# Pooled attention with a feed-forward layer: from the fourth chunk on, every engine's order is written out

## The chip, the cores and the metric

The kernel runs on one core of a Trainium2 chip. The metric is device microseconds of that core for one execution; lower is better. TensorE (PE) multiplies matrices into PSUM, VectorE (DVE) and ScalarE (ACT) copy and compute, GpSimd (POOL) computes in SBUF alone, and SyncE (SP) issues DMAs. Each engine works through its own list of instructions in order: one that waits for a semaphore holds back all that stand behind it on that engine.

## The reference

```python
# 8 batches, 8 heads, 576 positions, 64 columns a head; k and v are averaged over groups of 8 positions
k_p = k.reshape(B, H, Sp, pool, D).mean(axis=3)
v_p = v.reshape(B, H, Sp, pool, D).mean(axis=3)
scores = scale * np.matmul(q, k_p.transpose(0, 1, 3, 2))
scores = scores - np.max(scores, axis=-1, keepdims=True)
attn = np.exp(scores)
attn = attn / (np.sum(attn, axis=-1, keepdims=True) + 1e-09)
out = np.matmul(attn, v_p)
# 4608 tokens of 512 columns, then w_in 512 x 2048 and w_out 2048 x 512
x = out.transpose(0, 2, 1, 3).reshape(B * S, H * D)
h = x @ w_in
return np.maximum(0.01 * h, h) @ w_out
```

## The kernel before

The 4608 tokens are worked through in nine chunks of 512 columns, numbered 0 to 8. Each factor of a product is held as a high and a low part, and three matmuls (high by high, high by low, low by high) stand for one product at full precision.

Chunks 0 to 2 multiply x by w_in directly. From chunk 3 on (`FAST = 3`) a product of two 2 x 2 block matrices is made from seven block products instead of eight. The function `pair` does this for two column blocks of w_in at a time, eight pairs to a chunk. Its names: `chain` (in the bank `pv`) and `left` and `right` (halves of the bank `pu`) are PSUM areas; `held` and `h` are SBUF copies and sums of them. A product's six matmuls are lines 1168 to 1170. ACT copies `chain` to `held` (L1196, L1203, L1209), DVE adds `held` to `left` or `right` (L1198, L1210, L1220), and ACT and DVE split the result into `gh` and `gl` (L1189, L1191). The product with w_out is cut into tiles of 128 tokens, three matmuls each (`m2_tile`, L1074 to L1076, called fills here); `pair` takes them from a list and puts them between block products. Four block products read sums of weight blocks that stand in DRAM: `load_sums` fetches them, 512 KB at a time, into three buffers in turn (`streamed`, L1130, issued by ACT).

Attention for later chunks runs beside the products of a chunk, piece by piece. For a tile of 128 positions and a group of four heads: scores (`pss`, L560, PE), maxima (L568, DVE), four exponentials (L572, ACT), sums and reciprocals (L592, L593, DVE), normalised rows (`at`, L600 to L610, POOL). SP writes them to DRAM (`rows<-at`, L626) and reads them back in another layout (`blocks<-rows`, L635); DVE transposes `blocks` in squares of 32 (L643), ACT and DVE split them (L647 to L650), and PE multiplies them by v (`pa`, L692 to L697). `turn_x` then builds from x the seven operands of the next chunk (B11, B21, T2, T1, T3, T4, B22; a cast on ACT, L1161, and a difference on DVE, L1162, each).

The order on PE is the order of the code (`manual_schedule` for PE alone): `tick()` is called after each step of a pair and takes the next attention unit from a list, evenly spread over the chunk. The order on DVE, ACT, POOL and SP is set by the scheduler of the tile layer from its own estimates of time, with a few `issue_after` hints.

Of the kernel before, what the change touches and what calls it, by code (L numbers as in the profile page):

```python
# [20 lines left out]

@with_exitstack
def tile_pooled_attention_ffn(
# [9 lines left out]
    nc = tc.nc  # L35

# [14 lines left out]


# [57 lines left out]

# [50 lines left out]


# [30 lines left out]
    def convert(i, f):  # L193
# [3 lines left out]
        def head():  # L197
# [7 lines left out]

            after = casts[max(0, len(casts) - BEHIND)] if casts else anchor.get("act")
            with tc.issue_after(after.ins) if after else nullcontext():
# [3 lines left out]
            with tc.issue_after(behind.ins) if behind else nullcontext():  # L211
# [14 lines left out]

# [112 lines left out]
    def get_keys():  # L339
        for i in range(2):  # L340
            for c in range(2):
                r, y = 64 * i + 32 * c, slice(32 * c, 32 * c + 32)
# [9 lines left out]
    def turn_keys(b):  # L352
        kT = keys_values(b)[0]
        with tc.issue_after(anchor["gl"].ins):
            nc.vector.transpose(kblocks, kblocks)
# [6 lines left out]
    def load_v(b):  # L362
# [9 lines left out]
        def finish():  # L372
            pooled(nc.vector if b == 1 else nc.gpsimd, sums[:, 0:2], raws[0], P)
            with tc.issue_after(anchor["dve"].ins) if b == 0 else nullcontext():
# [6 lines left out]
    def raw_steps(b):  # L381
# [3 lines left out]
        def load(n):  # L385
# [4 lines left out]
            if n == 2:  # L390
                if b > 2:
                    put_keys(st["ks"])
# [15 lines left out]
        def add(n):  # L408
# [45 lines left out]
    def load_piece(b, j):  # L454
# [3 lines left out]
        for half in range(2):  # L458
            qb = two.tile([P, 2, PMAX], F32, tag="q", name=f"qb{b}_{j}_{half}")
            for h in range(4 * half, 4 * half + 4):  # L460
                for c in range(2):
# [5 lines left out]
            q_of[b, j, half] = qb  # L467
# [26 lines left out]
    def place_v(b, sums, rem):  # L494
        _, v_hi, v_lo, _ = keys_values(b)
        behind = [anchor[x] for x in ("gl", "gh")] if b == 1 else []
        with ExitStack() as order:
            for x in behind:
                order.enter_context(tc.issue_after(x.ins))
# [141 lines left out]
    def p_moved(b, j, g, ab):  # L641
        with tc.issue_after(anchor["gl"].ins):
# [117 lines left out]
    def attention(b):  # L760
# [34 lines left out]
        def step(kind, n):  # L795
            def f():
# [4 lines left out]
                with tc.issue_after(behind) if behind else nullcontext():  # L801
# [22 lines left out]
        def lv():  # L824
            if b == 1:
                with tc.issue_after(anchor["gl"].ins):
# [202 lines left out]


# [33 lines left out]
    def m2_tile(k, t):  # L1064
# [5 lines left out]
        if first:  # L1070
            accs[t] = ps_acc.tile([P, DM], F32, tag=f"acc{t}", name=f"acc{n}_{t}")
# [52 lines left out]
    def load_sums(q):  # L1124
# [5 lines left out]
        nc.scalar.dma_start(t.bitcast(F32), sums[q % len(sums)])  # L1130
# [33 lines left out]
    def product(c, p, out, a, b, start):  # L1164
        w, x = weights_of(c, p, a), operand[c, b]
        for kk in range(2):
# [3 lines left out]
            nc.tensor.matmul(out, w[1][kk], x[:, 0, kk], start=False, stop=kk == 1, **args)  # L1170

    def pair(n, c, p, at, fills):
# [5 lines left out]
        held = wts.tile([P, 3, HALF], F32, tag="w0_15", name=f"held{nm}")  # L1178
        h = wts.tile([P, 2, CH], F32, tag="w0_11", name=f"h{nm}")

        def fill(times=1):
            for _ in range(times):
                fills.pop(0)()

        def done(i, f, at):
            g = h[:, i, :]
            gh = three.tile([P, CH], F32R, tag="gh", name=f"gh{nm}_{f}")
            gl = three.tile([P, CH], F32R, tag="gl", name=f"gl{nm}_{f}")
            casts.append(nc.scalar.copy(gh, g))  # L1189
            anchor["gh"] = casts[-1]  # L1190
            anchor["gl"] = nc.vector.tensor_tensor(gl, g, gh.bitcast(F32), op=ALU.subtract)  # L1191
            gs[at] = gh, gl
            fills.extend(lambda t=t: m2_tile(at, t) for t in range(NT))

        product(c, p, chain, "A11", "B11", True)
# [3 lines left out]
        yield  # L1199
        fill(1 if p == 0 and c == FAST else 2)  # L1200
        yield
        product(c, p, chain, "S2", "T2", False)
        nc.scalar.copy(held[:, 1], chain)  # L1203
        product(c, p, right, "S1", "T1", True)
        yield
        fill(1 if p == 0 and c == FAST else 2)
        yield
# [3 lines left out]
        fill()  # L1211
        yield
        fill(2)
        yield
# [3 lines left out]
        done(1, 2 * p + 1, at + 1)  # L1218
        product(c, p, right, "S4", "B22", False)
        nc.vector.tensor_tensor(h[:, 0, HALF:], held[:, 1], right, op=ALU.add)  # L1220
        yield
        nc.scalar.activation(h[:, 0, :], h[:, 0, :], AF.Prelu, alpha=0.01)
        done(0, 2 * p, at)
        fill()
        yield
# [10 lines left out]
    def store(n, c, t, a):  # L1236
        if n == len(runs) - 1:
# [11 lines left out]
            return  # L1249
        o = five.tile([P, DM], F32, tag="o", name=f"o{n}_{t}")  # L1250
# [28 lines left out]
    def convert_to(n):  # L1279
        nonlocal stepped  # L1280
        while stepped < min(int(n), len(steps)):
            steps[stepped]()
            stepped += 1

# [50 lines left out]
    for n, (c, fs) in enumerate(runs):  # L1335
        us = list(units[n])
# [27 lines left out]
        if quick:  # L1364
            for p in range(NF // 2):
# [28 lines left out]
        if c == FAST - 1:  # L1394
            for m in range(4, len(NAMES)):
                turn_x(FAST, m)
            for qn in range(len(STREAM)):
                load_sums(qn)
    while fills:
# [33 lines left out]
```

## Time and profile before

| what | value |
|---|---|
| median of 3 runs | 1014.76 us (1010.26 to 1019.28) |
| the profiled execution, own time | 1018.58 us |
| its span, first to last instruction | 1016.7 us |
| start of chunk 3 (first block product) | 373.1 us |
| PE busy, share of the span | 914.8 us, 90% |
| DVE, ACT, POOL busy | 505.4, 498.7, 226.4 us |
| mean granted clock of TensorE | 0.971 |

The page gives busy times; the windows view cuts them by stretch, so that a chunk can be compared with the work in it. PE's matmuls overlap, so the length of one is not its cost: the distance between the starts of two that follow each other is. A waits view names, for each wait, the instruction that ended it, and the timeline shows the instructions of one engine in order of time.

### The profile page before, as it was taken

To read this page: it belongs to the slowest core of one execution; us is meant where nothing else is said; L and a number is where in the kernel's file an instruction comes from. 1 tells how busy PE (TensorE), PEld (TensorE's weight loads), DVE (VectorE), ACT (ScalarE), POOL (GpSimd) and SP (SyncE) were. 2 spreads that over 40 slices of the span, in tenths; PEclk is the share of its full clock that TensorE was granted. 3 is DMA by queue.
4 is the path that set the end of the run, shared out by engine and by line. 5 is a ranking of instruction groups with operands and counts; after the bars stand their busy time and mean duration, and the time that the engine had idled before them with its cause. 6 is when DMAs were issued, how large, how long until landed. Compare 5 with 4: busy or idle time off the path is not lost.

```text
span 1016.7 us, 15236 instructions
## 1 busy us (share of the span) xinstructions
PE 914.8 (90%) x5132; PEld 790.8 (78%) x5132; DVE 505.4 (50%) x1105; ACT 498.7 (49%) x1542; POOL 226.4 (22%) x366
## 2 busy tenths in 40 slices
PE   4988999998989997889979688878998899999998
PEld 3867788887768876778868577767877789898997
DVE  5798666244756654344445353443545444444222
ACT  4897755254434444434544344543555445444333
POOL 3022100434355411222113221134121111100000
PEclk9899999999989999899999898998999999999999
DMA  9995422334355927785578746887379636835442
GB/s 171 268 284 172 123 71 63 88 107 120 106 188 134 187 79 186 163 172 133 160 173 177 160 125 167 174 178 157 109 187 183 139 125 168 173 110 175 135 118 71
DMA packets 276694, 152.05 MB, mean 150 GB/s; under 512 B 229448, under 2 KB 240712, under 8 KB 276616
## 3 DMA queue, kind: packets, MB, share of 16 engines
q1 hardware_dynamic: 258760, 87.63, 39.4%
q10 hardware_dynamic: 17856, 63.45, 20.6%
q8 instruction: 41, 0.67, 0.3%
q14 instruction: 37, 0.30, 0.1%
HBM read 120.21 MB, written 30.82 MB: 149 GB/s over the span
## 4 chain that ended last, share of the span: by engine, by line
PE 49%; DMA 20%; SPq 8%; ACT 8%; DVE 7%; POOL 4%; issue 3%; ACTq 0%; DVEq 0%; POOLq 0%
PE acc L1074 8%; PE acc L1075 8%; PE acc L1076 7%; DMA blocks<-rows 6%; DMA rows<-at 4%; PE pv L1169 3%; PE pv L1168 3%; PE pv L1170 3%; ACT e L572 2%; PE pu L1168 2%; SPq L463 2%; PE ph L1050 2%; PE ph L1052 2%; PE ph L1051 2%; DMA vremraw<-in_v_dram 2%
## 5 line engine op out<-in xcount | busy, mean ns | idle before, releaser
L1074 PE MATMUL acc<-w,gh 128*128 128x512 f32 x576 | 235.3, 409 | 8.2 <-DVE o L1255 8.2
L1075 PE MATMUL acc<-w,gh 128*128 128x512 f32 x576 | 229.7, 399 | 0.0
L1076 PE MATMUL acc<-w,gl 128*128 128x512 f32 x576 | 228.1, 396 | 0.0
L1074 PEld LDWEIGHTS acc<-w,gh 128*128 128x128 f32 x576 | 111.1, 193 | 25.3 <-DVE o L1255 5.7
L572 ACT ACTIVATE e<-pss,red 128x72 f32<-128x72 f32 x320 | 98.5, 323 | 65.3 <-DVE red L568 64.2
L1076 PEld LDWEIGHTS acc<-w,gl 128*128 128x128 f32 x576 | 110.3, 191 | 25.1
L1075 PEld LDWEIGHTS acc<-w,gh 128*128 128x128 f32 x576 | 111.2, 193 | 14.3
L600 POOL TENSOR_TENSOR at<-e,red 128x128 f32<-128x128 f32 x100 | 42.4, 445 | 261.8 <-DVE red L593 137.1
L1168 PE MATMUL pv<-T,streamed 128*128 128x256 f32 x288 | 84.7, 294 | 9.7 <-ACT held L1196 6.5
L1191 DVE TENSOR_TENSOR gl<-h,gh 128x512 fp32r<-128x512 f32 x96 | 68.1, 713 | 40.7 <-ACT gh L1189 39.9
L1169 PE MATMUL pv<-T,streamed 128*128 128x256 f32 x288 | 82.2, 285 | 0.0
L1170 PE MATMUL pv<-T,streamed 128*128 128x256 f32 x288 | 81.9, 284 | 0.0
L1050 PE MATMUL ph<-x,w 128*128 128x512 f32 x192 | 79.2, 412 | 0.7 <-DVE gl L1060 0.7
L1052 PE MATMUL ph<-x,w 128*128 128x512 f32 x192 | 76.8, 400 | 0.6 <-DVE w L221 0.6
L1051 PE MATMUL ph<-x,w 128*128 128x512 f32 x192 | 76.7, 400 | 0.0
L1168 PEld LDWEIGHTS pv<-T,streamed 128*128 128x128 f32 x288 | 55.6, 193 | 18.5 <-ACT held L1196 9.3
L572 ACT ACTIVATION_READ_ACCUMULATOR e<-pss,red 128x1 f32 x320 | 66.3, 207 | 0.0
L1189 ACT CAST gh<-h 128x512 fp32r<-128x512 f32 x96 | 59.4, 624 | 10.1 <-DMA blocks<-rows 8.2
L1168 PE MATMUL pu<-T,streamed 128*128 128x256 f32 x96 | 30.0, 313 | 35.2 <-DVE h L1198 34.9
L1210 DVE TENSOR_TENSOR h<-held,pu 128x256 f32<-128x256 f32 x48 | 19.8, 412 | 83.5 <-ACT held L1209 83.4
L1169 PEld LDWEIGHTS pv<-T,streamed 128*128 128x128 f32 x288 | 55.6, 193 | 4.3
L1209 ACT COPY held<-pv 128x256 f32<-128x256 f32 x48 | 17.9, 374 | 78.4 <-PE pv L1170 78.4
(208 smaller groups left out, 2013.3 us busy)
## 6 DMA issues: line engine op xcount, KB each, us to landing
streamed<-sums ACTq DMA_DIRECT2D x120, 512.0 KB
w_bits<-in_moe_w_in_dram SPq DMA_DIRECT2D x16, 512.0 KB
w_bits<-in_moe_w_out_dram SPq DMA_DIRECT2D x16, 512.0 KB
sums<-sums SPq DMA_DIRECT2D x32, 256.0 KB
out_dram<-o SPq DMA_DIRECT2D x31, 256.0 KB
rows<-at SPq DMA_DIRECT2D x40, 192.0 KB
blocks<-rows SPq DMA_DIRECT2D x40, 120.0 KB
v0raw<-in_v_dram SPq DMA_DIRECT2D x16, 256.0 KB
```

The lines of the kernel that those rows point to most:

```text
L572: ins = nc.scalar.activation(e[:, h, :], scv[:, h, :], AF.Exp, bias=mx[:, h : h + 1], accum_out=sm[:, h : h + 1],)
L1050: nc.tensor.matmul(ph, w[:, 0, ks], xh[kk], start=kk == 0, stop=False)
L1051: nc.tensor.matmul(ph, w[:, 0, ks], xl[kk], start=False, stop=False)
L1052: nc.tensor.matmul(ph, w[:, 1, ks], xh[kk], start=False, stop=kk == NK - 1)
L1074: nc.tensor.matmul(a, gh[:, r], hi, start=first, stop=False)
L1075: nc.tensor.matmul(a, gh[:, r], lo, start=False, stop=False)
L1076: nc.tensor.matmul(a, gl[:, r], hi, start=False, stop=last)
L1168: nc.tensor.matmul(out, w[0][kk], x[:, 0, kk], start=start and kk == 0, stop=False, **args)
L1169: nc.tensor.matmul(out, w[0][kk], x[:, 1, kk], start=False, stop=False, **args)
L1170: nc.tensor.matmul(out, w[1][kk], x[:, 0, kk], start=False, stop=kk == 1, **args)
L1189: casts.append(nc.scalar.copy(gh, g))
L1191: anchor["gl"] = nc.vector.tensor_tensor(gl, g, gh.bitcast(F32), op=ALU.subtract)
```

## The change

From the first pair of chunk 3 on, DVE, ACT, POOL and SP are in manual order too. The list of units and `tick()` are not used there. Attention, the building of operands and the stores are cut into small tasks. A task names the tasks that it must follow and by how many places, and what it costs on ACT, DVE or SP; a pair has 15 places, `work` is called at each, and emits every task that is due and for which that place has room. A pair's own copies and additions are emitted at fixed places. The products' order in a pair is kept. `load_sums` is called in `product` and issued by SP instead of ACT; `held` and `h` are one buffer for all pairs; one Prelu reads two areas of `held`, and the split of the first column block is emitted in the next pair. `need` emits an operand's tasks just ahead of its product where they were not due yet. The core of the diff:

```diff
@@ load_sums @@
-        nc.scalar.dma_start(t.bitcast(F32), sums[q % len(sums)])
+        nc.sync.dma_start(t.bitcast(F32), sums[q % len(sums)])
@@ product @@
+        need(("T", c, b, 1))
...
+        if a in USED:
+            used = len(USED) * ((c - FAST) * (NF // 2) + p) + USED.index(a)
+            if used % 2:
+                load_sums(used // 2 + len(STREAM))
@@ pair @@
         product(c, p, chain, "A11", "B11", True)
         nc.scalar.copy(held[:, 0], chain)
+        if behind:
+            behind.pop(0)()
+        yield 1
         product(c, p, left, "A12", "B21", True)
-        nc.vector.tensor_tensor(h[:, 0, :HALF], held[:, 0], left, op=ALU.add)
+        nc.vector.tensor_tensor(held[:, 0], held[:, 0], left, op=ALU.add)
...
+    def may_go(name):
+        _, after, at, _, reader, cost = tasks[name]
+        if at > clock[0] or not all(gap_ok(x, d) for x, d in after):
+            return False
+        if reader and len(bankers) > 1 and not gap_ok(bankers[-2], 2):
+            return False
+        return all(room[x] > 0 for x in cost)
...
+    GRANTS = {
+        "act": {3: 9, 4: 6, 5: 6, 6: 6, 7: 6, 8: 2, 9: 6, 10: 6, 11: 6, 12: 3},
+        "dve": {1: 4, 3: 7, 4: 7, 5: 7, 6: 7, 7: 6, 8: 2, 9: 6, 10: 7, 11: 7, 12: 7, 13: 6},
+    }
+    FREE = (3, 4, 7, 8, 10, 11, 12, 15)
...
+    def work(at):
+        clock[0] += 1
+        for x, granted in GRANTS.items():
+            room[x] = min(room[x] + granted[at], 12) if at in granted and at not in (1, 3, 5, 9) else granted.get(at, 0)
+        room["sp"] = min(room["sp"] + 7, 7)
+        room["pe"] = int(at in FREE)
+        waiting_for = [x for x in tasks if x not in made]
+        for x in sorted(waiting_for, key=lambda x: tasks[x][3]):
+            if may_go(x):
+                emit(x)
...
+        task((*name, "put"), put, [((*name, "norm"), 3)], first=True, sp=5)
...
+        task((*name, "ld"), ld, [(x, 7) for x in last] + [((*before, "low"), 2)], first=True, sp=20)
+        task((*name, "turn"), turn, [((*name, "ld"), 13)], dve=11)
+        task((*name, "high"), high, [((*name, "turn"), 1)] + [((*before, "av", i), 1) for i in range(2)], act=7)
...
@@ the loop over chunks @@
+        if c == FAST:
+            by_hand.append(c)
+            order.enter_context(tc.manual_schedule(engines={e.engine for e in (nc.vector, nc.scalar, nc.gpsimd, nc.sync)}))
...
-                for i, _ in enumerate(pair(n, c, p, kf, fills)):
-                    if i in (3, 4, 5, 6, 7):
-                        used = len(USED) * ((c - FAST) * (NF // 2) + p) + i - 3
-                        if used % 2:
-                            load_sums(used // 2 + len(STREAM))
-                    tick()
+                for i in pair(n, c, p, kf, fills):
+                    work(i)
```

PE's list is the same up to the first block product of chunk 3. The other engines' lists up to there differ in the first three `streamed` loads, which now stand on SP, and in a few instructions of chunk 3 that the scheduler had drawn ahead into chunk 2 (transposes of q, parts of v) and that now stand behind. Three places of what follows show the change.

DVE in chunk 4, before: the transpose of the first `blocks` of batch 4's second piece, ahead of the third pair's second addition (`h4_2` is chunk 4, pair 2; L1198, L1210 and L1220 are the pair's additions).

```order
L355 STREAM_TRANSPOSE kblocks_119<-kblocks_119 128x384
L592 TENSOR_TENSOR red4_4_1_5142<-red4_4_1_5142,tiny_124 128x4
L1198 TENSOR_TENSOR h4_2_5151<-held4_2_5150,pu4_2_5149 128x256
L360 TENSOR_SCALAR kT_108<-kblocks_119 64x4x64
L360 TENSOR_SCALAR kT_108<-kblocks_119 64x4x8
L593 RECIPROCAL red4_4_1_5142<-red4_4_1_5142 128x4
L643 STREAM_TRANSPOSE blocks_134<-blocks_134 128x960
L1210 TENSOR_TENSOR h4_2_5151<-held4_2_5150,pu4_2_5149 128x256
```

The same transpose now (L1481), in chunk 4's second pair (the additions are L1225, L1246 and L1257 now):

```order
L1257 TENSOR_TENSOR held_3699<-held_3699,pu4_0_4887 128x256
L1211 TENSOR_TENSOR gl4_0_1_5043<-h_3700,gh4_0_1_5025 128x512
L1481 STREAM_TRANSPOSE blocks_134<-blocks_134 128x960
L1225 TENSOR_TENSOR held_3699<-held_3699,pu4_1_5055 128x256
L1211 TENSOR_TENSOR gl4_0_0_5076<-h_3700,gh4_0_0_5063 128x512
```

It still stands ahead of an addition (L1225), but 13 places behind the loads that it waits for.

SP at those loads, before: four `blocks<-rows` right behind two stores of rows.

```order
L626 DMA rows4_1_0_4891<-at4_4_0_5049 64x12x32
L626 DMA rows4_1_1_4987<-at4_3_1_5101 128x12x32
L635 DMA blocks_134<-rows4_1_0_4891 32x30x32 x4
L463 DMA qb5_1_0_5182<-in_q_dram 32x10x32 x4
L626 DMA rows4_1_1_4987<-at4_4_1_5168 64x12x32
```

Now the same loads are L650, with the `streamed` loads (L1144) between them and the stores (L641):

```order
L641 DMA rows4_1_0_4450<-at4_4_0_4813 64x12x32
L1144 DMA streamed22_4876<-sums2_138 128x1024
L641 DMA rows4_1_1_4681<-at4_3_1_4847 128x12x32
L650 DMA blocks_134<-rows4_1_0_4450 32x30x32 x4
L1144 DMA streamed23_4950<-sums3_139 128x1024
L279 DMA k0raw6_4970<-in_k_dram 64x2x512 x2
```

A `streamed` load waits for the product that last read its buffer, so SP now waits for PE there, and a store that waits holds the load behind it.

ACT at the start of chunk 4, before: the operand B21 is cast behind the first copy (L1196) of the last pair of chunk 3 (`held3_7`).

```order
L1222 ACTIVATE h3_6_4573<-h3_6_4573 128x512
L1189 CAST gh3_6_12_4675<-h3_6_4573 128x512
L1196 COPY held3_7_4684<-pv3_7_4682 128x256
L1161 CAST B21_4_4754<-xw4_1_4115 128x512
L708 COPY xw4_1_4115<-pa4_0_2_4700 128x256
```

Now it is cast behind the first copy (L1220) of chunk 4's first pair, whose second product reads B21 (`pu4_0`):

```order
L1259 ACTIVATE h_3700<-held_3699 128x512
L1220 COPY held_3699<-pv4_0_4886 128x256
L1206 CAST gh3_7_14_4895<-h_3700 128x512
L1650 CAST B21_4_4898<-xw4_1_4247 128x512
L1650 CAST T2_4_4917<-turned4_4691 128x512
```

B21 of chunk 4 moved from a pair ahead of its first product to just ahead of it; for chunks 5 to 8 it stands in the pair before.

## Rows read from the trace of the kernel before

**Rows 1.** The page, part 2: granted clock of TensorE in 40 slices, in tenths.

```profile
PEclk9899999999989999899999898998999999999999
```

**Rows 2.** Windows, chunk 3 to chunk 8: stretch, busy us by engine, clock, DMA share, GB/s.

```profile
373.00:486.50 113.50, 99.38 (x590) 88.22 (x589) 45.72 (x103) 49.67 (x159) 26.02 (x44) 0.94 0.69 156
486.50:606.20 119.70, 99.05 (x603) 88.30 (x602) 53.51 (x118) 53.88 (x178) 28.60 (x51) 0.96 0.71 160
606.20:725.30 119.10, 100.61 (x603) 88.48 (x602) 51.09 (x118) 53.54 (x178) 29.15 (x52) 0.94 0.69 161
725.30:830.80 105.50, 96.99 (x603) 85.39 (x602) 51.24 (x116) 53.46 (x176) 18.34 (x34) 1.00 0.65 155
830.80:921.30 90.50, 89.97 (x570) 81.40 (x569) 38.45 (x80) 45.27 (x132) 11.23 (x21) 1.00 0.58 150
921.30:1017.00 95.70, 91.33 (x559) 81.67 (x557) 25.80 (x51) 33.62 (x75) 0.00 (x0) 1.00 0.39 122
```

**Rows 3.** Windows, the last chunk's first pair (PE, PEld, DVE, ACT, POOL busy).

```profile
921.30:931.80 10.50, 10.50 (x67) 9.52 (x66) 3.54 (x8) 4.16 (x11) 0.00 (x0) 1.00 0.35 105
```

**Rows 4.** Waits of PE, 373 to 831 us: us in total, times, longest.

```profile
PE pu L1168 <- DVE h L1198: 34.4, 14, 7.1
```

**Rows 5.** Timeline of DVE, chunk 4's third pair: start, us, instruction, idle before it.

```profile
517.59 0.41 DVE L1198 TENSOR_TENSOR h<-held,pu 128x256 f32<-128x256 f32 x1
...
526.24 1.18 DVE L643 STREAM_TRANSPOSE blocks<-blocks 128x960 f32<-128x960 f32 x1 [7.62 <-DMA blocks<-rows]
527.35 0.38 DVE L1210 TENSOR_TENSOR h<-held,pu 128x256 f32<-128x256 f32 x1
```

**Rows 6.** Timeline of PE, the same pair and the next.

```profile
523.84 0.28 PE L1170 MATMUL pv<-T,streamed 128*128 128x256 f32 x1
527.78 0.39 PE L1168 MATMUL pu<-B,streamed 128*128 128x256 f32 x1 [3.67 <-DVE h L1210]
...
532.84 0.31 PE L692 MATMUL pa<-pT_hi,v_hi 128*128 128x320 f32 x1
532.98 0.31 PE L695 MATMUL pa<-pT_lo,v_hi 128*128 128x320 f32 x1
```

**Rows 7.** Waits of DVE and of SP's queue, 373 to 831 us.

```profile
DVE blocks L643 <- DMA blocks<-rows: 46.6, 11, 7.6
...
SPq L626 <- POOL at L610: 134.1, 21, 28.0
```

**Rows 8.** Groups of PE by form, 373 to 921 us: count, busy us, mean ns, idle before.

```profile
L560 PE MATMUL pss<-kT,qT 128*128 128x144 f32 x176 | 29.7, 293 | 0.0
...
L692 PE MATMUL pa<-pT_hi,v_hi 128*128 128x256 f32 x20 | 5.6, 280 | 0.0
L692 PE MATMUL pa<-pT_hi,v_hi 128*128 128x320 f32 x16 | 5.2, 326 | 0.0
```

**Rows 9.** The chain that ended last: two pieces of PE, start and us.

```profile
498.14 0.49 PE pss L560 x4
...
498.63 0.12 PE pv L1168
...
501.00 0.23 PE acc L1075
```

**Rows 10.** Windows of L560 alone, chunks 6 and 7 (PE, PEld).

```profile
725.30:830.80 105.50, 6.53 (x40) 5.95 (x40) 1.00 0.65 155
830.80:921.30 90.50, 3.92 (x24) 3.66 (x24) 1.00 0.58 150
```

**Rows 11.** Groups of ACT and DVE, 373 to 921 us.

```profile
L1196 ACT COPY held<-pv 128x256 f32<-128x256 f32 x40 | 15.1, 377 | 3.6 <-PE pv L1170 3.6
...
L1161 ACT CAST B<-xw 128x512 fp32r<-128x512 f32 x15 | 9.3, 619 | 0.2
...
L1162 DVE TENSOR_TENSOR T<-turned,T 128x512 fp32r<-128x512 f32 x20 | 13.8, 698 | 5.0 <-ACT T L1161 4.4
```

**Rows 12.** Timeline of SP: the four loads of `blocks` that DVE waits for in rows 5.

```profile
518.88 2.10 SPq L635 DMA_DIRECT2D blocks<-rows  x4
```

More of the change, by code (lines that the diff above doesn't have):

```diff
@@ L383, in raw_steps, with load @@
         st = {}
-        def load(n):
+        def load(n, keep=True):
             if n == 0:
@@ L406, in load, with add @@
             st["r", 1] = load_main(b, v, 0, "v")
-        def add(n):
+        def add(n, part=None):
+            if part is not None:
+                if n == 0:
+                    if part == 0:
+                        st["ks"] = one.tile([P, NK, D], F32, tag="ksum", name=f"ksum{b}")
+                    pooled(nc.gpsimd, st["ks"][:, 2 * part : 2 * part + 2], st["r", part], P)
+                elif n == 1 and part == 0:
+                    st["vs"] = one.tile([P, NK, D], F32, tag="vsum", name=f"vsum{b}")
+                    pooled(nc.gpsimd, kremsum[:64, :, 0, :], st["r", 0][:, 0:1, :], 64)
+                elif n == 1:
+                    pooled(nc.gpsimd, st["vs"][:, 0:2], st["r", 1], P)
+                elif part == 0:
+                    st["rem"] = one.tile([P, 1, D], F32, tag="vremsum", name=f"vremsum{b}")
+                    pooled(nc.gpsimd, st["vs"][:, 2:4], st["r", 0], P)
+                else:
+                    pooled(nc.gpsimd, st["rem"], st["r", 1][:, 0:1, :], P)
+                return
             if n == 0:
@@ L466, in load_piece @@
                     )
-            q_of[b, j, half] = qb
     def turn_q(b, j, t):
@@ L1210, in pair @@
         nc.vector.tensor_tensor(h[:, 1, HALF:], held[:, 2], right, op=ALU.add)
[L1211 to L1214, printed above, removed]
+        yield 9
+        for i in range(10, 13):
+            fill()
+            yield i
         product(c, p, chain, "A22", "T4", False)
@@ new lines, in pair, with task @@
+        rest(1, 2 * p + 1, at + 1, gh)
+        nc.scalar.activation(
+            h[:, 0, :].rearrange("p (x y) -> p x y", x=2), held[:, 0:2], AF.Prelu, alpha=0.01
+        )
+        got = []
+        behind.append(lambda: got.append(rounded(0, 2 * p, at)))
+        behind.append(lambda: rest(0, 2 * p, at, got[0]))
+        yield 14
+        fill()
+        yield 15
+    clock, made, tasks, room, bankers = [0], {}, {}, {"act": 0, "dve": 0, "sp": 0, "pe": 0}, []
+    def task(name, fn, after=(), at=0, first=False, reader=None, rank=1, **cost):
+        assert name not in tasks, name
+        tasks[name] = fn, tuple(after), at, 0 if first else rank, reader, cost
@@ new lines, in emit, with gap_ok @@
+    def emit(name):
+        fn, _, _, _, reader, cost = tasks[name]
+        made[name] = clock[0]
+        for x, y in cost.items():
+            room[x] -= y
+        if reader:
+            bankers.append(reader)
+        fn()
+    def gap_ok(name, gap):
+        return name not in tasks or (name in made and made[name] + gap <= clock[0])
+    def may_go(name):
[5 more added lines that the diff above has]
+        return all(room[x] > 0 for x in cost)
@@ new lines, in need @@
+    def need(name):
+        if name not in tasks or name in made:
+            return
+        _, after, _, _, reader, _ = tasks[name]
+        for x, _ in after:
+            need(x)
+        if reader and len(bankers) > 1:
+            need(bankers[-2])
+        emit(name)
+    GRANTS = {
[3 more added lines that the diff above has]
+    FREE = (3, 4, 7, 8, 10, 11, 12, 15)
@@ new lines, in work, with store_late, copy, keep @@
+    def work(at):
[8 more added lines that the diff above has]
+                emit(x)
+    def store_late(c, t, a):
+        got = []
+        r = 2 * S - 2 * TAIL + (c - 2) * CH + t * P
+        def copy():
+            i = t // 2
+            if t % 2 == 0:
+                ends[c, i] = one.tile([P, 2, DM], F32, tag=f"X{i}", name=f"o{c}_{i}")
+            o = ends[c, i][:, t % 2]
+            nc.scalar.copy(o[:, : DM // 2], a[:, : DM // 2])
+            nc.vector.tensor_copy(o[:, DM // 2 :], a[:, DM // 2 :])
+            got.append(o)
+        def keep():
+            o = got[0]
+            if c == 2 and t == 0:
+                for b in range(2):
+                    nc.sync.dma_start(out[b * S + CH : (b + 1) * S, :], o[TAIL * b : TAIL * (b + 1), :])
+            else:
+                nc.sync.dma_start(out[r : r + P, :], o)
+        task(("o", c, t), copy, [(("o", c, t - 1), 0)] if t else [], clock[0] + 1, True, act=4, dve=4)
+        task(("st", c, t), keep, [(("o", c, t), 1)], 0, True, sp=5)
@@ L1398, in tile_pooled_attention_ffn @@
                 load_sums(qn)
+    for x in behind:
+        x()
     while fills:
```

361 lines of the change are left out of this document (327 added, 34 removed).

## The prediction

> **What bounds the kernel now.** The page's clock line comes first: TensorE's granted clock falls below full in several slices after the first third and in none of the last third's until the end [rows 1]. Then the windows, cut at the first block product of each chunk: PE is busy for 90 us of chunk 7's 90.5, but chunks 3 to 5 take 113.5 to 119.7 us with some 100 us of busy PE, and their clock is 0.94 to 0.96 [rows 2]. No other engine is near its limit: DVE and ACT are busy for some 50 of 120 us, and the DMA engines for 0.7 of it.
>
> How much of this is PE's own work? A pair in the last chunk, with nothing beside it, takes 10.5 us at full clock with PE busy throughout [rows 3], so eight take 84.0. Attention adds 176 score matmuls, four to a group, 0.49 us a group: 44 x 0.49 = 21.6 us. It adds 36 groups of four matmuls for `pa`; 20 of them are 256 wide at 0.12 us a start, like a block product's, and 16 are 320 wide, which start 0.14 us apart: 20 x 4 x 0.12 + 16 x 4 x 0.14 = 18.6 us [rows 6, 8, 9]. Chunk 3's first pair has two fills less, six matmuls of 0.23 us, 1.4 us. Chunks 3 to 7 thus hold 5 x 84.0 + 21.6 + 18.6 - 1.4 = 458.8 us of PE at full clock. They take 113.5 + 119.7 + 119.1 + 105.5 + 90.5 = 548.3 us. **89.5 us** are lost there, and that is all a new order can win; PE's work is not touched.
>
> Where do they go? The waits view puts 34.4 us of idle PE, in 14 waits of up to 7.1 us, on one addition of DVE, L1198 [rows 4]. The addition itself takes 0.41 us. DVE's own longest wait says why: 46.6 us at the transpose of `blocks`, until the DMA landed [rows 7]. One case stands in the rows. DVE finishes chunk 4's third L1198 at 518.0, then comes to the transpose, and is idle for 7.62 us until 526.24; L1210 behind it runs at 527.35 [rows 5], and PE, which ended its last product at some 524.1, goes on at 527.78 [rows 6]. The waiting instruction needed nothing of PE, but stood in front of what PE needed. Such a stop is paid twice, since the clock is lower after it: 0.06, 0.04 and 0.06 of three chunks are up to 6.8 + 4.8 + 7.1 = 18.7 us of the 89.5 [rows 2].
>
> **The change, part by part.** *The place of the transpose.* The four loads were issued at 518.88 and had landed at 526.24, 7.4 us later [rows 5, 12]. Now at least 13 places lie between them and the transpose. A pair with some attention is 11 to 12 us and has 15 places, so 13 are about 10 us: 2.6 us to spare if SP issues the loads on time. The order shows the transpose still ahead of an addition, so a late load would still stop PE; the distance alone does the work. PE has two fills and a product, 4 x 0.23 + 2 x 0.23 + 6 x 0.12 = 2.1 us, between the product that L1198 adds and the one that waits for it, so a delay of DVE up to about 2 us costs nothing.
>
> *The rest of DVE and ACT.* Their work is the same. A chunk without stops would be some 94 us long; chunk 6 holds 51.2 us of DVE and 53.5 of ACT [rows 2], so each would be busy for 0.55 to 0.57 of it. What is left of small waits can be bounded by rows. Chunk 7 has 24 of 176 score matmuls [rows 10] and that share of the attention, 24/176 x 40.2 = 5.5 us, and takes 90.5 - 84.0 - 5.5 = 1.0 us too long. Chunk 6 has 40, or 9.1 us, and takes 105.5 - 84.0 - 9.1 = 12.4 us too long at full clock. For chunks 3 to 6 the residue is thus 1.0 x 40/24 = 1.7 us a chunk at the low end (7 us in all) and 12.4 at the high end (50). Most of chunk 6's is the same trouble with the transposes, so I take a value near the low end, **3 us a chunk, 12 us**, and 1 us for chunk 7.
>
> *B21 of chunk 4.* Here the change adds a wait. The operand is cast on ACT behind the copy of the product just before its own. From the end of that product: copy 0.37, the cast of `gh` 0.62 (the size of L1161's), the cast of B21 0.62, the difference on DVE 0.70 [rows 11], and some 0.3 for handing over: **2.6 us** of idle PE, once. The later chunks have the operand a pair ahead: nothing.
>
> *The streamed loads on SP.* PE waits for no load in the rows of before, while ACT issued them. On SP a load stands behind all that SP waits for. Its time: the buffer is read again one pair later, 10.5 us less a product of 0.7, so 9.8 us for SP to reach it, and to land. SP's largest wait now is for POOL's rows: 134.1 us over 21 waits, 6.4 on average, 28.0 at most [rows 7]. An average one fits; the longest would cost 28.0 - 9.8 = 18 us. These waits come where DVE or ACT hold POOL up, and go with the stops; a store of rows now follows its row by three places, 2 us. I take nothing, between 0 and the 18 us of one such wait. ACT loses 20 issues a chunk, which it did not wait for: nothing.
>
> The Trainium skill ("DMA: Bandwidth & Descriptors", rules for kernel authors) says that spreading DMAs over the issuing engines saves sequencer time alone, since all run on the same 16 engines. By that rule the move costs SP only the issuing. The 28.0 us wait in the row differs on one point that the rule leaves out: an issuer that waits for another engine holds its own loads back.
>
> *The sum.* In the profiled execution's own time: 1018.6 - 89.5 = 929.1, plus 12 + 1 + 2.6 = 15.6, gives **945 us**. That execution was 3.8 us above the median. As the loss was measured in the same execution, I subtract nothing. Without any residue it is 929; with the high end of the residue (50 + 1 + 2.6) 983.
>
> **The rivals.**
>
> *Half of the stops stay.* The loads come late because SP is late (its rows, its waits), and DVE waits again at every other transpose. 18 transposes stand in chunks 3 to 6 and 7's start; each one at half of the longest wait seen, 7.6/2 = 3.8 us, less 2.1 us of cover, is 1.7 us, 31 us in all, and some 6 us of lower clock with them. 945 + 37 = 982 us. For it: the transpose is still in front of additions. Against it: 2.6 us to spare, and the pairs without a stop in the trace of before.
>
> *No difference.* The waits move to other places in the pair: each of ACT's copies and DVE's additions stands between two products, and the fixed order leaves an engine idle where the scheduler found something to do. If that costs 2 us a pair, 32 pairs give back 64 us and the result is 1009. Against it: 10.5 us pairs at full clock are made of the same steps [rows 3].
>
> *Slower.* One mechanism: SP as the only issuer. It waits for POOL's rows, DVE's stores, landed rows and now for PE's products, all in one list. If it stands still for 13 us in each pair instead of the 6.4 on average [rows 7], every streamed load is 3.2 us later than its 9.8 us, and PE stops for that in each of 32 pairs: 102 us, and 945 + 102 = 1047. It decides from 89.5 - 15.6 = 74 us, or 2.3 us a pair: above that the kernel is slower.
>
> The Trainium skill has a rule on this side as well ("DMA: Bandwidth & Descriptors", queues, rings and completion order): an engine takes the rings of its queues in turn, and one ring's descriptors in order. By it the streamed loads lose a ring of their own and stand behind what SP issued before. No run here shows it yet; with DMA shares of 0.7 it would add to this rival, and its price is in the 2.3 us above.
>
> **How the numbers follow.** Forecast (930 to 962): 0.64. Half of the stops (962 to 1004): 0.23. No difference: 0.05. Slower: 0.08. Within 1% of 1014.8 (1004.6 to 1024.9) a measurement of this kernel can hardly tell a change from none, as its three runs lie 0.9% apart. So faster by over 1%: 0.64 + 0.23 = 0.87; within: 0.05; slower: 0.08. The range that holds 0.8 begins at 931, just above no residue, and takes in the half case's 982 and the high residue's 983: up to 985.
>
> **What would show it.** In the changed kernel's windows, chunks 4 to 6 should be 95 to 100 us long at clock 1.00, and chunk 3 about the same, since a part of the attention now comes earlier. In the waits, DVE at the transpose for `blocks<-rows` should be under 10 us, and PE for L1225 a few us. At chunk 4's start PE should wait some 2.6 us for B21. PE waiting for `streamed` would speak for the slow rival, long waits at the transpose for the half one. The prediction is wrong if the matmuls themselves are slower when DMAs and four engines run without a pause, since 458.8 us rests on rows of quiet stretches.

## The result and the profile after

The kernel became faster: 950.21 us (median of 4 runs, 949.61 to 951.84) against 1014.12 us (median of 4, 1010.26 to 1019.28), a ratio of 0.937 with an interval of 0.933 to 0.941. The profiled execution took 950.41 us, with a span of 948.6 us. The forecast was 945 us, 5 us too low, and its range (931 to 985) holds the result.

The page of the changed kernel, parts 1 and 2: busy us, share of the span and instructions of each engine; and the granted clock in 40 slices, to be held against [rows 1].

```profile
PE 896.7 (95%) x5132; PEld 781.6 (82%) x5132; DVE 506.6 (53%) x1105; ACT 492.3 (52%) x1542; POOL 224.0 (24%) x366
...
PEclk9899999999999999999999999999999999999999
```

DVE, ACT and POOL are busy for the same time as before (505.4, 498.7 and 226.4 us there). PE is busy 18.1 us less (914.8 before) with the same work. Most of that fits the clock: what it lacks to full over chunks 3 to 5 came to 18.7 us before and is 4.1 us now (0.02 of chunks 3 and 4), and no slice of the changed part is below 0.9 any more.

The windows of the changed kernel, chunk 3 to chunk 8, answer to [rows 2] (length, busy us of PE, PEld, DVE, ACT, POOL, clock, DMA share, GB/s).

```profile
371.50:472.30 100.80, 96.08 (x612) 86.73 (x611) 48.39 (x115) 52.35 (x193) 26.12 (x52) 0.98 0.85 184
472.30:575.50 103.20, 97.49 (x606) 87.08 (x605) 62.13 (x133) 57.17 (x194) 42.06 (x66) 0.98 0.95 214
575.50:671.30 95.80, 94.60 (x601) 85.35 (x602) 49.19 (x114) 52.21 (x169) 23.80 (x43) 1.00 0.76 180
671.30:767.00 95.70, 95.06 (x606) 86.10 (x605) 52.55 (x118) 54.93 (x187) 15.73 (x37) 1.00 0.80 177
767.00:853.30 86.30, 85.82 (x539) 77.46 (x537) 29.43 (x56) 34.79 (x81) 3.60 (x4) 1.00 0.44 136
853.30:949.00 95.70, 91.34 (x559) 81.67 (x557) 25.62 (x51) 32.51 (x76) 0.00 (x0) 1.00 0.39 121
```

The five chunks last 481.8 us instead of 548.3, 66.5 us less. Chunk 3 also begins 1.6 us earlier, and the last one has its old length. That is the whole difference of the spans, 1016.7 - 948.6 = 68.1 us. Chunks 3 to 5 won most (12.7, 16.5 and 23.3 us), as they had lost most. The DMA share rose to 0.85 and 0.95 in chunks 3 and 4: the new order brings attention's transfers earlier, and chunk 7 has fewer of them.

Waits of the changed kernel, 371 to 853 us: for each engine and line what it waited for, us in total, times, longest. First PE, to be held against [rows 4].

```profile
PE pu L1183 <- DMA streamed<-sums: 3.8, 2, 3.0
PE pv L1184 <- DVE T L1656: 1.7, 1, 1.7
PE pu L1183 <- ACT B L1650: 1.6, 1, 1.6
PE pv L1183 <- DMA streamed<-sums: 1.4, 3, 0.7
PE pv L1183 <- ACT h L1252: 1.2, 1, 1.2
PE pv L1581 <- DVE vremparts L1575: 1.1, 1, 1.1
PE pu L1183 <- DVE held L1257: 0.5, 1, 0.5
```

There is no wait for the pair's first addition any more (L1225, once L1198 with 34.4 us). Five short ones for `streamed` are new, 5.2 us together. The same view for DVE and for SP's queue answers to [rows 7].

```profile
DVE blocks L1481 <- DMA blocks<-rows: 13.7, 5, 5.4
```

```profile
SPq L1144 <- PE pv L1185: 99.4, 36, 5.7
SPq L1144 <- PE pu L1185: 49.8, 23, 4.6
...
SPq L641 <- POOL at L625: 9.2, 6, 3.7
```

DVE's wait at the transpose fell from 46.6 to 13.7 us. SP's for POOL's rows fell from 134.1 to 9.2 us; it now stands waiting for PE's products instead, 149.2 us in 59 waits, since the loads of `streamed` are its own. The case of [rows 5] and [rows 12], in chunk 4's second pair now: SP's four loads, and DVE's timeline (start, us, instruction, idle before it).

```profile
478.34 2.48 SPq L650 DMA_DIRECT2D blocks<-rows  x4
```

```profile
490.45 1.17 DVE L1481 STREAM_TRANSPOSE blocks<-blocks 128x960 f32<-128x960 f32 x1
491.73 0.42 DVE L1225 TENSOR_TENSOR held<-held,pu 128x256 f32<-128x256 f32 x1
```

12.1 us lie between the issue and the transpose, which starts without a wait, and the addition follows at once. Before, DVE came to it early, stood for 7.62 us and the addition with it.

### The profile page after: what moved, and what is told of

Read it like the earlier page. It is cut to its first block, busy times and chain, and to the rows that moved or that the text cites. A ratio compares the mean times of both kernels' runs of the same rounds, so it can differ in the third digit from the quotient of the medians.

```text
span 948.6 us, 15313 instructions
## 1 busy us (share of the span) xinstructions
PE 896.7 (95%) x5132; PEld 781.6 (82%) x5132; DVE 506.6 (53%) x1105; ACT 492.3 (52%) x1542; POOL 224.0 (24%) x366
## 5 line engine op out<-in xcount | busy, mean ns | idle before, releaser
L1090 PEld LDWEIGHTS acc<-w,gl 128*128 128x128 f32 x576 | 108.9, 189 | 24.6
L1088 PEld LDWEIGHTS acc<-w,gh 128*128 128x128 f32 x576 | 109.8, 191 | 13.3
L1089 PEld LDWEIGHTS acc<-w,gh 128*128 128x128 f32 x576 | 109.8, 191 | 12.4
L1183 PE MATMUL pv<-T,streamed 128*128 128x256 f32 x288 | 82.1, 285 | 1.7 <-DMA streamed<-sums 1.4
L1184 PE MATMUL pv<-T,streamed 128*128 128x256 f32 x288 | 81.4, 283 | 1.7 <-DVE T L1656 1.7
L1185 PE MATMUL pv<-T,streamed 128*128 128x256 f32 x288 | 81.3, 282 | 0.0
L1246 DVE TENSOR_TENSOR h<-held,pu 128x256 f32<-128x256 f32 x48 | 20.1, 420 | 111.9 <-ACT held L1245 111.9
L1257 DVE TENSOR_TENSOR held<-held,pu 128x256 f32<-128x256 f32 x48 | 20.1, 419 | 78.7 <-PE pu L1185 78.6
L1183 PEld LDWEIGHTS pv<-T,streamed 128*128 128x128 f32 x288 | 54.5, 189 | 8.6 <-ACT held L1245 1.1
L1184 PEld LDWEIGHTS pv<-T,streamed 128*128 128x128 f32 x288 | 54.6, 189 | 6.5 <-DVE T L1656 1.9
```

The source lines that it names most:

```text
L1088: nc.tensor.matmul(a, gh[:, r], hi, start=first, stop=False)
L1089: nc.tensor.matmul(a, gh[:, r], lo, start=False, stop=False)
L1090: nc.tensor.matmul(a, gl[:, r], hi, start=False, stop=last)
L1183: nc.tensor.matmul(out, w[0][kk], x[:, 0, kk], start=start and kk == 0, stop=False, **args)
L1184: nc.tensor.matmul(out, w[0][kk], x[:, 1, kk], start=False, stop=False, **args)
```

## The experiments

Each kernel was timed together with the kernel before on the same chip; a ratio below is against that, with its 95% interval. "The changed kernel" is the one that gave 0.937. Differences from it in us are differences of medians; the kernel before, timed each time, had medians from 1013.4 to 1016.7 us, so they are good to some 3 us.

**1 and 2. Less distance between the loads and the transpose.** 13 places become 6, then 10. Nothing else differs in the rules, though tasks that follow the transpose move up with it.

```diff
-        task((*name, "turn"), turn, [((*name, "ld"), 13)], dve=11)
+        task((*name, "turn"), turn, [((*name, "ld"), 6)], dve=11)
```

> The 13 places between the loads of blocks and their transpose are cut to 6, some 4.7 us where the loads took 7.4 us in the trace of before. Theory D (the gain is the distance: DVE no longer stands in front of PE's additions waiting for a DMA): DVE's wait at the transpose grows from 13.7 us to 40 us or more, PE waits for the additions again, TensorE's clock falls in places, 965 to 990 us. Rival A (the gain comes from the rest: small tasks with room for each engine, no issues on ACT): 948 to 953 us.

Measured with 6: 971.65 us, 0.959 (0.956 to 0.962), 21.4 us slower than the changed kernel. DVE's waits at the transpose and one of them on its timeline, with the addition behind it:

```profile
DVE blocks L1481 <- DMA blocks<-rows: 56.3, 13, 9.6
```

```profile
506.05 1.18 DVE L1481 STREAM_TRANSPOSE blocks<-blocks 128x960 f32<-128x960 f32 x1 [9.55 <-DMA blocks<-rows]
507.16 0.38 DVE L1257 TENSOR_TENSOR held<-held,pu 128x256 f32<-128x256 f32 x1
```

```profile
PE pu L1183 <- DVE held L1257: 15.0, 6, 7.0
```

This is the picture of [rows 4] and [rows 5] again, at another addition. Chunks 3 to 5 have clocks of 0.97, 0.95 and 0.94, and chunk 4 takes 112.4 us. DVE waits longer at the transposes than in the kernel before (56.3 us against 46.6), and yet this kernel is 42 us faster than that one: the seven places are worth 21 of the 64 us, and the larger part of the gain does not hang on them.

> 10 places instead of 13, some 7.8 us. B21 of chunk 4 is then ready a pair ahead, so the stop of about 5 us at the start of chunk 4 goes. Theory D: DVE's wait at the transposes grows a little, below what PE has in cover: 943 to 950 us. If 13 places are needed under the denser DMA traffic: 952 us or more.

Measured with 10: 965.97 us, 0.953 (0.949 to 0.957). DVE waits for 32.9 us in 8 waits, PE for L1225 12.5 us in 4 waits, and once for ACT's copy of `pa`, which stood behind ACT's wait for a transpose:

```profile
PE pu L1183 <- DVE held L1225: 12.5, 4, 6.7
PE pa L1504 <- ACT xw L1514: 8.3, 1, 8.3
```

B21 of chunk 4 is not waited for any more, as was expected, but the chunk takes 116.4 us. So the time falls with the distance, 971.7, 966.0, 950.2 us at 6, 10 and 13 places. Why ten places, some 7 to 8 us, are not enough, although 7.4 us lay between issue and landing in [rows 5, 12], can be read from SP. The longest wait, SP's four loads first and then DVE's transpose:

```profile
501.09 5.89 SPq L650 DMA_DIRECT2D blocks<-rows  x4
```

```profile
510.16 1.18 DVE L1481 STREAM_TRANSPOSE blocks<-blocks 128x960 f32<-128x960 f32 x1 [8.42 <-DMA blocks<-rows]
```

DVE came to the transpose at 501.74, before SP had issued the fourth load (506.98), and started it 3.2 us behind that issue. In [rows 5, 12] these were 5.3 us. Four of the eight waits, 26.4 of the 32.9 us, began before the fourth load was issued; and in all eight the transpose started 2.9 to 3.8 us behind the last issue, in the eleven waits of the kernel before 3.3 to 8.1 us. So the landing did not take longer in the denser traffic. SP came late to the loads and was slow in issuing them, 5.89 us for four instead of 2.10; what held it there no run shows.

**3. The `streamed` loads back on ACT**, at the same places of the program.

```diff
-        nc.sync.dma_start(t.bitcast(F32), sums[q % len(sums)])
+        nc.scalar.dma_start(t.bitcast(F32), sums[q % len(sums)])
```

> The streamed loads are issued by ACT again, at the same places. Theory S (SP as the only issuer, and one ring for all, costs the 5.2 us that PE waits for streamed in the changed kernel): these waits go, 943 to 948 us. Rival: ACT, which now waits for PE's product at each issue, passes that on: 952 us or more. Neither: 949 to 951 us.

Measured: 964.32 us, 0.952 (0.949 to 0.955), 14.1 us slower, as the rival had it. PE's waits for `streamed` are gone, but it waits for ACT instead (`h` 6.0 us in 5 waits, others of 1 to 2 us), and SP for POOL's rows again:

```profile
SPq L641 <- POOL at L625: 78.1, 19, 13.6
```

Chunk 3 also starts 4.3 us later (375.8; in experiment 11, again with ACT as the issuer, 1.7 us), and chunk 4 takes 108.9 us.

**4. No limits on what a place may hold of ACT and DVE.**

```diff
-            room[x] = min(room[x] + granted[at], 12) if at in granted and at not in (1, 3, 5, 9) else granted.get(at, 0)
+            room[x] = 99
```

> Every place has room for all tasks that are due; distances stay. Theory B (the room per place matters: without it DVE and ACT get several tasks in a row ahead of a pair's copies and additions): PE waits for held and h in many pairs, 960 to 1000 us. Theory D alone: the distances do the work, 946 to 953 us.

Measured: 968.17 us, 0.956 (0.952 to 0.959), 18.0 us slower. The limits are worth that much, but not in the way that the theory of the budget (B) had it, as guards of the pair's own additions. PE's largest waits are these:

```profile
PE pv L1183 <- DMA streamed<-sums: 6.1, 3, 3.9
PE pu L1183 <- DMA streamed<-sums: 4.7, 2, 4.1
PE pu L1183 <- DVE held L1257: 2.4, 1, 2.4
PE pa L1504 <- ACT e L1439: 2.2, 4, 0.7
```

One addition of 2.4 us is among them. `streamed` has 10.8 us, twice the changed kernel's 5.2, attention's own operands have most of the rest, and the clock of chunk 3 is 0.95 at a DMA share of 0.93 (0.98 and 0.85 in the changed kernel). Tasks that may go early bring their transfers early, and these meet the streamed loads. That is what the rows suggest; no run spread the transfers with the limits away.

**5, 6 and 10. Parts of the change in the kernel before**, under the scheduler's order: the `streamed` loads on SP alone (5), two more empty units between the loads of `blocks` and their transposes in the list of units (6), and both (10).

```diff
-        nc.scalar.dma_start(t.bitcast(F32), sums[q % len(sums)])
+        nc.sync.dma_start(t.bitcast(F32), sums[q % len(sums)])
```

```diff
-            out.extend(x for x in behind[:1] if x)
...
+            out.extend(x for x in behind[:1] if x)
+            put("-", "-")
...
-            put("-", f"pm{j}0")
+            put("-", "-", "-", f"pm{j}0")
```

> The kernel before with one part of the change alone: the streamed loads issued by SP, order left to the scheduler. Theory A2 (from the run with ACT as the issuer, 14 us slower: an ACT that waits for PE at each issue holds its other work back): part of the gain comes with this alone, 985 to 1008 us. The slow rival of the prediction (SP's waits for POOL, 6.4 us on average, delay the loads): PE waits for streamed, 1020 to 1060 us. Neither: 1009 to 1019 us.

> The kernel before with one part of the change alone: two more empty units stand between the loads of blocks and their transpose in the list of units, order still the scheduler's. Theory D (distance is the gain): DVE's wait of 46.6 us at the transposes shrinks, 970 to 1000 us. Rival: the scheduler puts the transposes where it sees room whatever the list says, or the later attention stops a chunk's start: 1005 us or more.

> The kernel before with two parts of the change: two more empty units between loads and transposes, and streamed issued by SP; order the scheduler's. Theory P (the parts add up, and the hand order of the rest is worth little): 970 to 995 us. Theory O (without the order written out, each wait taken away comes back elsewhere, as it did with either part alone): 1000 to 1020 us.

Measured: 1009.87 us, 0.994 (0.991 to 0.997), by its time neither of the two theories; 1019.52 us, 1.004 (1.002 to 1.006), as the rival had it; 1007.72 us, 0.991 (0.988 to 0.994). Waits of the first, the loads on SP alone, from an execution of 1017.15 us, the longest of its ten:

```profile
PE pu L1168 <- DMA streamed<-sums: 20.8, 4, 9.3
PE pu L1168 <- DVE h L1198: 11.2, 7, 3.7
PE pv L1168 <- DMA streamed<-sums: 6.8, 3, 4.4
```

The wait for L1198 fell from 34.4 to 11.2 us, but 27.6 us of waits for `streamed` took its place: this is the mechanism of the slow rival, and it takes back all that was won in this execution. The longest of these waits, on SP and on PE:

```profile
758.20 7.91 SPq L463 DMA_DIRECT2D qb<-in_q_dram  x15
766.20 1.35 SPq L1130 DMA_DIRECT2D streamed<-sums  x3
```

```profile
770.23 0.55 PE L1168 MATMUL pu<-T,streamed 128*128 128x256 f32 x1 [9.29 <-DMA streamed<-sums]
```

Fifteen loads of `qb` stood ahead of the `streamed` loads in SP's list. Once the first of these was issued, PE went on 4.0 us later. Waits of the second, with the empty units:

```profile
PE pu L1169 <- DVE h L1199: 21.0, 15, 3.5
PE pv L1169 <- ACT held L1197: 10.7, 6, 4.1
PE pv L1169 <- ACT h L1217: 7.9, 2, 4.6
```

DVE's wait at the transpose nearly halved there, to 26.7 us, and the time did not fall; PE stops for ACT's copies and in many short waits for the addition instead. With both parts `streamed` still has 22.8 us and an ACT copy 8.7 us. The theory that it takes the whole order (O) held: the issuer and as much distance as two empty units give, in the scheduler's order, are worth 9 us of the 64. A distance that takes the waits at the transposes away was not reached in that order.

**7 and 8. The start of chunk 4.** In the first pair of chunk 4 the two fills that stood behind the second product stand ahead of it, and B21's tasks ahead of them (7); with that, score groups every 12 places instead of 11 (8).

```diff
+        first = p == 0 and c == FAST + 1
+        if first:
+            need(("T", c, "B21", 1))
+            fill()
+            fill()
...
-                at += 4 if m < 2 else 11
+                at += 4 if m < 2 else 12
```

> The changed kernel with two fills of chunk 4's first pair put between the first product and the one that reads B21, and B21's tasks emitted ahead of them. Theory: the stop at chunk 4's start (1.6 + 0.3 us for B21, 1.7 us for T2, 1.2 us behind ACT) loses what the two fills cover, 1.4 us at most: 948 to 950 us. If the stop only moves to T2: 950 us, no change.

> As the kernel with the moved fills, and a score group is due every 12 places instead of 11, so that attention's transfers spread over more of chunks 4 to 7. Theory: what is left is PE waiting for streamed under full DMA engines (share 0.95 in chunk 4): 943 to 948 us. Rival: the waits fall in chunk 3, where the pace is the same: 948 to 951 us.

Measured: 950.54 us, 0.937 (0.934 to 0.939), no difference from the changed kernel; 948.01 us, 0.935 (0.932 to 0.938), which can't be told from it either. B21 is hardly waited for any more (0.5 us in 7, 1.9 us before), but T2, the operand cast right behind it, now is, 1.8 us at the next product in 7 and 8, and T3 0.6 and 0.4 us instead of 1.7. `streamed` has 5.5 us in both, and 948.01 us lies where the ranges of 8's two theories meet. Covering the first of two operands that are cast together moved the stop to the second.

**9. The pair's copies and additions behind the tasks of their place.** Every `yield` of `pair` moves ahead of the copies, additions or Prelus that it followed (six of these).

```diff
+        yield 1
         nc.scalar.copy(held[:, 0], chain)
         if behind:
             behind.pop(0)()
-        yield 1
```

> The changed kernel, but a pair's copies and additions are emitted behind the attention tasks of their place instead of ahead of them. Theory F (the fixed places matter: an engine must come to them first): PE waits for held and h at many products, 960 us or more. Theory D with cover (2 us of fills hide one place's tasks): 949 to 954 us.

Measured: 947.63 us, 0.932 (0.929 to 0.935). The theory of the fixed places (F) fell, and the time is below the range of D as well: with the products' own copies behind the tasks the kernel is not slower, and its median is the lowest of all, though the intervals overlap. `streamed` has 3.7 us of waits, the transpose 13.0 us. Tasks as small as these apparently delay a copy by less than PE's cover for it.

**11 and 12. ACT as issuer, at better places.** If ACT lost its time at the loads because they wait for a product (W), a load behind a copy that has just waited for the same or a later product would cost its issue alone. 12 adds the edits of 8.

```diff
-                load_sums(used // 2 + len(STREAM))
+                due.append(used // 2 + len(STREAM))
...
         nc.scalar.copy(held[:, 1], chain)
+        load_due()
```

> The changed kernel with streamed issued by ACT, but each issue stands right behind a copy or Prelu of ACT that waits for the same or a later product, so that the issue itself adds no wait for PE. Theory W (the 14 us of the run with ACT as the issuer came from the wait in front of the issue): 943 to 951 us, no PE wait for streamed. Theory I (they came from the issues' own time, 0.33 us each): 958 to 966 us.

> As the run before, with chunk 4's moved fills and 12 places between score groups. If theory W holds: 941 to 948 us, below the changed kernel. If not: 955 us or more.

Measured: 963.06 us, 0.948 (0.945 to 0.951), and 961.40 us, 0.946 (0.943 to 0.949): some 11 to 13 us slower than the changed kernel, so W in this form fell. Both times lie in the range of I, the issues' own time: 100 issues of 0.34 us are 34 us of ACT. But ACT's timeline shows that such a load waits for something else as well (line numbers are 5 to 9 higher in this kernel):

```profile
402.38 0.37 ACT L1251 COPY held<-pv 128x256 f32<-128x256 f32 x1 [1.72 <-PE pv L1185]
405.90 0.34 ACTq L1144 DMA_DIRECT2D streamed<-sums  x1
406.29 0.32 ACT L1448 ACTIVATE e<-pss,red 128x72 f32<-128x72 f32 x1 [3.54 <-DMA qb<-in_q_dram]
```

The copy ended at 402.75, its product was done, and the load still left at 405.90, released by the landing of a transfer of `qb`, which SP issues and no instruction of ACT reads. The exponentials stood behind it. All waits of ACT that ended with a landing of SP's transfers, in 370 to 870 us, come to 26.4 us in 15 waits (4.5 us in two more ended with a `streamed` load); the changed kernel has none. The largest, and PE's largest wait:

```profile
ACT e L1448 <- DMA qb<-in_q_dram: 6.7, 2, 3.5
```

```profile
PE pss L1433 <- ACT e L1448: 6.0, 2, 3.0
```

In the trace, 79 of the 100 loads that ACT issues there wait for one of eight semaphores with which the transfers of both SP and ACT report their landing. That explains a wait for another queue's transfer; a kernel with semaphores of its own for ACT's loads was not tried, so this cause is read, not shown, and no run tells it from the issues' own time.

## Why the prediction was right, and where it was off

**The loss and where it went.** Right. The prediction counted 458.8 us of PE's own work and 89.5 us lost. The chunks now take 481.8, so 23.0 us are still lost, against the 15.6 that it kept. In the profiled execution's own time that makes 1018.6 - 89.5 + 23.0 = 952.1, less the 1.6 us by which chunk 3 starts earlier: 950.5, and 950.41 was measured. To subtract nothing for the 3.8 us by which the execution before was above its median agrees with that: the gain is 68.1 us between the profiled spans and 64 between the medians.

**The place of the transpose.** Right as a mechanism, and shown by experiments 1 and 2 in the changed kernel; too large as a share, for the prediction named no other large source of the gain. With 6 places, and 56.3 us of waits at the transposes, 42 of the 64 us are still there. The margin was mis-sized: the "2.6 us to spare" held "if SP issues the loads on time", and it often does not, as experiment 2 shows. DVE still waits 13.7 us in five waits at 13 places. Four of these are 1.8 to 2.5 us long, about the cover of 2 us that the prediction gave PE; the longest, 5.4 us, stood ahead of L1246, and PE had other work until then. Experiment 6 adds what the prediction did not say: two more units of distance without the rest of the order are worth nothing.

**The residue of 3 us a chunk, 12 us for chunks 3 to 6.** The sum was somewhat too small and the spread wrong. With the prediction's own prices and the matmuls of each chunk (56, 44, 40, 36 and 0 score matmuls, 8, 8, 8, 10 and 2 groups for `pa`) PE's own work is 93.6, 93.5, 93.0, 93.6 and 85.0 us, so the losses are 7.2, 9.7, 2.8, 2.1 and 1.3 us. Chunks 5 and 6 are below the 3, chunks 3 and 4 far above. Of the 21.8 us of chunks 3 to 6, 1.9 are B21's and 5.2 those of the `streamed` loads; 14.7 stand against the 12. That a value near the low end fits is in part luck. The prediction took it because most of the 12.4 us of chunk 6 were to be the trouble with the transposes, but in that chunk (725 to 831 us) PE's waits before were 8.3 us in all, 4.9 of them for L1198, and DVE's at the transposes 4.8.

**B21 of chunk 4, 2.6 us.** The wait is there with 1.55 + 0.34 us, and with it came one that was not named: T3, three operands on, for which PE stops 1.67 us at 484.14. (The expectations above call it T2; but T2's product, at 479.06, and T1's ran without a wait, and 482.09 begins T3's.) The start of chunk 4, as it stands on PE's timeline, and DVE ahead of T3's difference:

```profile
474.74 0.38 PE L1183 MATMUL pu<-B,w 128*128 128x256 f32 x1 [1.55 <-ACT B L1650]
475.46 0.58 PE L1184 MATMUL pu<-B,w 128*128 128x256 f32 x1 [0.34 <-DVE B L1656]
...
484.14 0.39 PE L1184 MATMUL pv<-T,streamed 128*128 128x256 f32 x1 [1.67 <-DVE T L1656]
```

```profile
480.25 2.46 DVE L1552 TENSOR_SCALAR kT<-kblocks 64x256 f32<-64x256 f32 x2
482.74 0.77 DVE L488 STREAM_TRANSPOSE qT<-qb 128x256 f32<-128x256 f32 x2
483.44 0.65 DVE L1656 TENSOR_TENSOR T<-turned,T 128x512 fp32r<-128x512 f32 x1
```

The prediction costed one operand; another one, whose difference stands on DVE behind attention's work, is late in the same pair.

**The `streamed` loads on SP, taken at nothing, between 0 and 18 us.** This term was mis-sized: PE waits 5.2 us for them, and the clock is lower behind the longest of these waits, 2.97 us at 431.62. The 9.8 us that the prediction left for SP and the landing were enough but for five loads. Three of the waits, 4.1 us, fall in chunks 3 and 4, where the DMA share is 0.85 and 0.95 instead of the 0.7 that it had reckoned with; that the share is the cause no run shows. That spreading DMAs over the issuing engines saves sequencer time alone (the Trainium skill, "DMA: Bandwidth & Descriptors", rules for kernel authors) agrees with the landing, which takes as long on either queue, but not with the price: the same loads on ACT cost 11 to 14 us more (experiments 3, 11 and 12). That one ring's descriptors are taken in order (the Trainium skill, "DMA: Bandwidth & Descriptors", queues, rings and completion order) can't be seen to have cost anything here: by the packets in the traces a load takes 3.2 us in the median from the end of its issue to its last packet, on SP's queue (changed kernel) and on ACT's (experiment 3). What delays the loads in experiment 5 is their late issue; in the longest wait of the changed kernel the landing was slow as well, 5.2 us.

**"ACT loses 20 issues a chunk, which it did not wait for: nothing."** This step failed. With ACT as issuer again the kernel is 14.1 us slower (experiment 3), although PE's 5.2 us for `streamed` vanish: in the order by hand, freeing ACT is worth more than the loads on SP cost. ACT did wait at some of them in the kernel before. There 13 of its waits, 35.7 us in 370 to 870 us, ended with a landing of SP's transfers, and in seven of these, 17.3 us, it stood at a `streamed` load, as here:

```profile
764.95 0.33 ACTq L1130 DMA_DIRECT2D streamed<-sums  x1
765.32 0.62 ACT L1189 CAST gh<-h 128x512 fp32r<-128x512 f32 x1 [3.20 <-DMA blocks<-rows]
```

With SP as issuer such waits for any landing are 4.1 us in experiment 5 and none in the changed kernel. The prediction, which looked at PE's waits alone, did not read that view. The sum does not show the error, since it takes the whole loss as gone, whatever caused it: for the kernel of experiment 3 the same working would give 945 us too, against 964.32 measured. In this the closeness of the forecast is luck.

**The rivals.** Half of the stops would have shown long waits at the transpose; 13.7 us in five is three tenths of before, and PE's waits name an addition once, with 0.5 us (L1257), at a place where DVE had not waited at a transpose. No difference and slower did not come, but the slow rival's mechanism is real: in the scheduler's order it costs 27.6 us (experiment 5). In the order by hand the store of a row follows its row by three places, SP's wait for POOL falls to 9.2 us, and the loads come in time but for five.

**What was expected to be seen.** Chunks 5 and 6 are in the forecast 95 to 100 us at clock 1.00; chunks 3 and 4 are not, with 100.8 and 103.2 us at 0.98. DVE's wait at the transposes is 13.7 us, not under 10, and PE's wait for L1225, put at a few us, did not come. The matmuls themselves did not become slower with all engines at work: chunk 6 is within 2.1 us of the prices from quiet stretches, at a DMA share of 0.80.

What stays lost is thus some 12.6 us of waits of PE as the view sums them, up to 4 us at the lower clock (0.02 of chunks 3 and 4), and small gaps. No version that was run is clearly better than the changed kernel: 8 and 9 have medians 2 to 3 us lower, with overlapping intervals.

## What to carry to other kernels

On an engine that works in order, an instruction that waits for a transfer belongs behind the transfer by more than its landing time: the delay of the engine that issues the transfer comes on top, and a new order changes it. Here 13 places held where 10 did not, although the landing had not become longer. When transfers are moved to another issuing engine, count what each issue waits for, its hidden waits for other transfers too, the issue's own time (0.34 us, a hundred times here), and who stands behind it. An operand that is made just in time brings the next ones of its list with it, so to cover the first alone moves the stop to the second.

## What the runs showed of the hardware that was not expected

A stop of PE does not always cost clock. The windows right behind three stops of the changed kernel: the one of 1.55 us at 474.74, the one of 1.67 us at 484.14, and the one of 2.97 us at 431.62 (the number ahead of the DMA share is the granted clock).

```profile
474.70:479.00 4.30, 3.92 (x12) 3.24 (x13) 2.76 (x6) 1.33 (x4) 0.00 (x0) 0.60 0.94 258
...
484.10:488.40 4.30, 4.26 (x27) 3.86 (x28) 2.65 (x7) 2.17 (x7) 1.77 (x4) 1.00 0.62 157
...
431.60:436.00 4.40, 4.38 (x23) 4.11 (x24) 1.02 (x2) 0.81 (x2) 0.00 (x0) 0.68 1.18 156
```

Behind the first and the third the clock was at its lower level, 1.2 GHz, for most of the stretch; behind the second, as long as the first (which had 0.34 us more right behind it), it stayed at 2.4 GHz. What decides between them these runs do not show. At the lower level the products' matmuls started 0.21 us apart instead of 0.12.

And a load issued by ACT waited for landings of SP's transfers whose data it has nothing to do with, 26.4 us in all in experiment 11, as told there.
